# A fused attention and mixture-of-experts kernel: the first unit's second layer by parts, and the second mixture ahead of its loop

## The chip, the cores and the metric

The kernel runs on one core of a Trainium2 chip. The metric is device time in microseconds (us) of one execution. The time before is the median of three runs. Engines are named as in the profile: PE is TensorE (matmuls) and PEld its weight loads, DVE is VectorE, ACT is ScalarE, POOL is GpSimd, SP is SyncE, whose queue issues the DMAs; a name with a q behind it (SPq, PEldq) is the engine's sequencer.

## What is computed

Three stages follow each other: Nystrom attention, a gated layer, and a mixture of experts with a skip.

```python
def _attn_ref(q, k, v):                     # 4 x 8 heads, 576 tokens, 64 wide
    q_lm, k_lm = means of 18 neighbours     # 32 landmarks
    A, Bm, C = sm(q, k_lm), sm(q_lm, k_lm), sm(q_lm, k)
    Z = ...                                 # six steps of an iterative inverse of Bm
    return A @ Z @ C @ v

def _moe_ref(x, w_gate, w_val, w_out, rms_g):
    xn = x / sqrt(mean(x * x) + 1e-6) * rms_g
    g = xn @ w_gate                         # 512 -> 1536
    return (g * sigmoid(g) * (xn @ w_val)) @ w_out

def _moe2_ref(x, w_skip, w_gate, w1, w2):   # 8 experts
    do_compute = x @ w_skip > 0             # the other tokens are passed through
    e = argmax(x @ w_gate); p = softmax(x @ w_gate)[e]
    return x + p * (relu(x @ w1[e]) @ w2[e])
```

The first is in outline; the routing picks one expert for each token that is computed. The gated layer's weights come as 64-bit floats and are converted on the chip.

## The kernel before

The 2304 tokens are four batches of 576, and each batch is two **units** of 288 tokens. `run_unit(u)` (line 1179) does the gated layer of one unit: for each of twelve parts f of the hidden layer two groups of matmuls (`gemm`, into the PSUM tiles pg and pv) and their evictions, which leave a high and a low half in h_t; then the second layer. `project(c, ps, fs)` (line 875) adds parts fs of the hidden layer to output chunk c, one of four, in PSUM tile o, with three matmuls for each part (high by high, high by low, low by high). PSUM tiles pg, pv, o, ph and py share one pool of four banks (`accbank`).

The **second layer's weights** w_out are loaded and converted during unit 0, part by part (`convert_wout`, line 761: one load, operations on ScalarE and VectorE, then a high half from ScalarE and a low half from VectorE or GpSimd, alternately). In unit 0 all conversions left are named first (`drain(conv)`, line 1188), then the four chunks one after the other, each with all twelve parts, with a `slot()` after two parts.

`slot` (line 1161) lets side work (the conversions, the next batch's attention and weight products, the last unit's finish) be named between the matmuls. `Paced` adds up an estimate of each engine's busy time, and a slot stops as soon as an engine is more than SLACK = 700 ahead of TensorE. The order in which an engine runs its instructions is then laid down at compile time by a scheduler that goes by the order of naming and by when inputs are ready; each engine runs its own list in order.

The **mixture of experts** goes by pairs of an expert and a batch. `list_pairs` (line 968) makes a list of those that have tokens, with their number at its end (index 2 LP). `early` does this during unit 7, for the first three batches, so that one pair is known; `list_pairs("rest", ...)` lists the others when unit 7 is finished. `pair_at` loads an entry into registers of SyncE. `mixture(e, b, nxt, ahead)` (line 1084) does one pair with all 576 tokens of the batch: eight parts of a hidden layer (w2 of the pair split into halves, 24 matmuls into ph for each half of the tokens, then Relu on ScalarE and the low half on VectorE), the loads of the pair's routing weights mc and of the rows of the output (`load_rows`, line 1054), the loads and splits of the next pair's x and w1 and the loads of its w2, then the output matmuls (py), which VectorE scales by mc and adds to the rows, and the stores. mc is 0 for tokens that the pair doesn't serve.

The first pair runs as straight-line code; a loop over the others follows (`tc.For_i`, line 1337), whose count each engine loads into a register (`number`, line 1005). Between two passes of the loop stands a back edge, at which the engines wait for each other. Nearly all instructions carry line 58, that of a helper; loads and loop instructions have their own lines.

Of the kernel before, what the change touches and what calls it, by code (L numbers as in the profile page):

```python
# [62 lines left out]
def attention_moe_kernel(  # L63
# [75 lines left out]
    def accbank(name):  # L139
        return acc.tile([128, 512], F32, name=name, tag="acc")  # L140

    def bank(name):
        return pb.tile([128, 512], F32, name=name, tag="b")
# [824 lines left out]
    def list_pairs(name, but=None):  # L968

        pq = bank("pq")  # L970
        PE.matmul(
            pq[0:32, 0:1], Ms.rearrange("p b e -> p (b e)"), ones[:, 0:1],
            start=True, stop=True,
        )
        fl = rt.tile([32, 1], F32, name="fl")
        if but is None:
            V.tensor_scalar(fl, pq[0:32, 0:1], 0.0, None, ALU.is_gt)
        else:
            V.scalar_tensor_tensor(
                fl, pq[0:32, 0:1], 0.0, but, ALU.is_gt, ALU.subtract  # L980
            )
        pq = bank("pq")
        PE.matmul(pq[0:32, 0:1], tri, fl, start=True, stop=True)
        ps = rt.tile([32, 1], F32, name="slot")
        V.tensor_copy(ps, pq[0:32, 0:1])
        oh = const.tile([32, LP], F32, name=f"oh{name}")
        V.tensor_scalar(oh, pos, ps, fl, ALU.is_equal, ALU.mult)
        pl = bank("pl")
        PE.matmul(pl[0:1, 0:LP], pair[:, 1:2], oh, start=True, stop=True)
        PE.matmul(pl[0:1, LP : 2 * LP], pair[:, 2:3], oh, start=True, stop=True)  # L990
        PE.matmul(
            pl[0:1, 2 * LP : 2 * LP + 1], fl, ones[0:32, 0:1], start=True, stop=True
        )
        lst = const.tile([1, 2 * LP + 1], I32, name=name)
        V.tensor_copy(lst, pl[0:1, 0 : 2 * LP + 1])
        return lst, oh[:, 0:1]

    SPE = mybir.EngineType.SP

# [5 lines left out]
    def number(lst):  # L1005
        return nc.values_load(lst[0:1, 2 * LP : 2 * LP + 1], min_val=0, max_val=B * E)

    def pair_at(lst, i):
        return ld(lst, i, E - 1), ld(lst, i + LP, B - 1)
# [44 lines left out]
    def load_rows(e, b):  # L1054

        mc = late.tile([128, 5], F32, name="mc")
        mrow = m_d[bass.ds(b * S, S), bass.ds(e, 1)]
        with nc.allow_non_contiguous_dma(reason="one column"):
            SP.dma_start(
                mc[:, 0:4], mrow[0:512].rearrange("(t p) o -> p (t o)", p=128)  # L1060
            )
            SP.dma_start(mc[0:64, 4:5], mrow[512:576])
        orow = out[bass.ds(b * S, S), :]
        olds = []
        for t in range(5):
            m = 128 if t < 4 else 64
            old = late.tile([128, DM], F32, name=f"old{t}")
            SP.dma_start(old[0:m], orow[128 * t : 128 * t + m, :])
            olds.append(old)
        return mc, orow, olds  # L1070

    def early(res):

        lst, res["mark"] = list_pairs("lst")
        e, b = res["pair"] = pair_at(lst, 0)
        for c in range(KC):
            load_x(b, c, V if c % 2 else G)
        yield
        for i in range(2):
            for f in range(4 * i, 4 * i + 4):  # L1080
                load_w1(e, f, V if f % 2 else G)
            yield

    def mixture(e, b, nxt, ahead):

        hs = []
        for f in range(FC2):
            if ahead:
                r = w2raw(f)
            else:  # L1090
                r = late.tile([128, S], F32, name="w2r", tag="ld", bufs=4)[:, 0:DM]
                load_w2(e, f, r)
            rsplit(V if f % 2 else G, *w2s(f), r)
            wh, wl = (t.rearrange("p (c f) -> p c f", c=KC) for t in w1s(f))

            hh, hx, hl = (
                hroom[f][:, s] for s in (slice(0, S), slice(512, 640), slice(640, None))
            )
            for t in range(2):
                ts = slice(NH * t, NH * t + NH)  # L1100
                ps = accbank("ph")[:, 0:NH]
                for c in range(KC):
                    xh, xl = xs[0][:, c, ts], xs[1][:, c, ts]
                    PE.matmul(ps, wh[:, c], xh, start=(c == 0), stop=False)
                    PE.matmul(ps, wh[:, c], xl, start=False, stop=False)
                    PE.matmul(ps, wl[:, c], xh, start=False, stop=(c == KC - 1))
                A.activation(hh[:, ts], ps, AF.Relu)
                n = (NH, 512 - NH)[t]
                V.scalar_tensor_tensor(
                    hl[:, NH * t : NH * t + n], ps[:, 0:n], 0.0,  # L1110
                    hh[:, NH * t : NH * t + n].bitcast(F32), ALU.max, ALU.subtract,
                )
            V.scalar_tensor_tensor(
                hx[:, 64:128], ps[:, n:NH], 0.0, hx[:, 0:64].bitcast(F32),
                ALU.max, ALU.subtract,
            )
            hs.append((hh, hx, hl))
            if f == FC2 - 3:
                mc, orow, olds = load_rows(e, b)
            yield  # L1120
        en, bn = nxt()
        if not w2r_t:
            w2r_t.extend(wo_tile(F32) for _ in range(FC2 // 2))
        for c in range(KC):
            load_x(bn, c, V)
        for f in range(FC2):
            load_w1(en, f, V if f % 2 else G)
        for f in range(FC2):
            load_w2(en, f, w2raw(f))

        ps = accbank("py")
        for f in range(FC2):
            for i, w in enumerate(w2s(f)):
                PE.matmul(
                    ps, hs[f][1], w,
                    start=(f + i == 0), stop=(f + i == FC2),
                )
        old = olds[4][0:64]
        for p in (ps[0:64], ps[64:128]):
            V.scalar_tensor_tensor(old, p, mc[0:64, 4:5], old, ALU.mult, ALU.add)  # L1140
        SP.dma_start(orow[512:S, :], old)
        yield
        for t in range(4):
            ts = slice(128 * t, 128 * t + 128)
            old = olds[t]
            ps = accbank("py")
            for f in range(FC2):
                (hh, _, hl), (wh, wl) = hs[f], w2s(f)
                PE.matmul(ps, hh[:, ts], wh, start=(f == 0), stop=False)
                PE.matmul(ps, hh[:, ts], wl, start=False, stop=False)  # L1150
                PE.matmul(ps, hl[:, ts], wh, start=False, stop=(f == FC2 - 1))
            V.scalar_tensor_tensor(
                old, ps, mc[:, t : t + 1], old, ALU.mult, ALU.add
            )
            SP.dma_start(orow[ts, :], old)
            yield
# [4 lines left out]
    def slot():  # L1161

        for n in "VAG":
            busy[n] = max(busy[n], busy["P"])
        for g in side[:]:
            if max(busy[n] for n in "VAG") > busy["P"] + SLACK:
                break
            if next(g, "end") == "end":
                side.remove(g)

    def drain(g):
        for _ in g:
            pass
        if g in side:
            side.remove(g)
# [3 lines left out]
    def run_unit(u, before):  # L1179

        for f in range(FC):
            before(f)
            h = hidden_g(gemm(u % 2, f, "g"))
            slot()
            hidden_v(f, h, gemm(u % 2, f, "v"))
            slot()
        if u == 0:
            drain(conv)
        elif fin:
            drain(fin.pop())  # L1190
        x2T = x2T_tile(F32)
        for c in range(KC):
            ps = accbank("o")[:, 0:NH]
            for f in range(0, FC, 2):
                project(c, ps, (f, f + 1))
                slot()
            evacuate(x2T, c, ps)
        fin.append(finish(u, x2T))
        side.insert(0, fin[0])
# [117 lines left out]

    def others():
        yield from fin[0]
        rest.append(list_pairs("rest", first["mark"])[0])  # L1320
        yield

    oth = others()
# [2 lines left out]
    for g in side[:]:  # L1326
        drain(g)

    def after_first():
        drain(oth)  # L1330
        return pair_at(rest[0], 0)

    for _ in mixture(*first["pair"], after_first, False):
        next(oth, None)
        next(oth, None)
    npairs = number(rest[0])
    with tc.For_i(0, npairs) as i:  # L1337
        e, b = pair_at(rest[0], i)
        drain(mixture(e, b, lambda: pair_at(rest[0], i + 1), True))
    ph1.close()  # L1340
    ctx.close()

# [32 lines left out]
```

## Time and profile before

| | |
|---|---|
| median of 3 runs | 715.3 us (713.17 to 715.6) |
| the profiled execution | 715.35 us |
| its span in the trace | 713.6 us |
| mean granted clock of TensorE | 0.958 |
| TensorE busy | 651.2 us (91%) |
| VectorE busy | 471.5 us (66%) |
| ScalarE busy | 294.9 us (41%) |
| GpSimd busy | 145.6 us (20%) |

The profiled execution is longer than its span by 1.75 us, which lie around it. Times in the trace count from the start of the span. The granted clock is a share of full speed, 2.4 GHz; the other level is 1.2 GHz. The chain of waits follows what ended last back to what released it; a timeline merges neighbouring instructions of a kind and gives in brackets how long the engine was idle before them and what ended that.

### The profile page before, as it was taken

What the parts mean: (1) busy time and instruction counts of PE and PEld (TensorE: products, weight loads), DVE (VectorE), ACT (ScalarE), POOL (GpSimd) and SP (SyncE); (2) the same over time, 40 slices, a digit from 0 to 9 for tenths busy, and PEclk for the clock granted to TensorE, in tenths of its full rate; (3) what the DMA queues carried; (4) which work ended last, traced back from release to release, by engine and by line L of the source; (5) the groups of instructions that cost most, each with busy time, mean ns of one, the idle gap of its engine ahead of it and who ended that gap; (6) DMA issues with size and microseconds to landing.
All of it is one profiled execution on the core that took longest, in us unless ns stands there. A gap on an engine that the chain in (4) does not pass through costs nothing. (4 is left out here: it accounts for less than half of the span.)

```text
span 713.6 us, 13229 instructions
## 1 busy us (share of the span) xinstructions
PE 651.2 (91%) x4891; PEld 562.2 (79%) x4891; DVE 471.5 (66%) x1012; ACT 294.9 (41%) x637; POOL 145.6 (20%) x162
## 2 busy tenths in 40 slices
PE   5388599798999799999999999999999999997997
PEld 4366267687977598978898888999899988986985
DVE  6985999988987775888458968360634464352451
ACT  1864888834224421442441434340533253332240
POOL 4000035304200140320130230040542033022120
PEclk9766799999999999999999999999999999998999
DMA  9775644671246651229612208310641474372344
GB/s 310 244 238 204 222 180 153 196 186 51 88 99 134 187 133 51 84 75 206 159 36 67 80 6 178 93 37 1 184 127 63 147 234 148 106 235 81 119 143 160
DMA packets 79434, 97.10 MB, mean 136 GB/s; under 512 B 16016, under 2 KB 58000, under 8 KB 79376
## 3 DMA queue, kind: packets, MB, share of 16 engines
q1 hardware_dynamic: 79376, 96.33, 45.8%
q8 instruction: 36, 0.59, 0.3%
q14 instruction: 22, 0.18, 0.1%
HBM read 76.97 MB, written 19.34 MB: 135 GB/s over the span
## 5 line engine op out<-in xcount | busy, mean ns | idle before, releaser
L58 PE MATMUL o<-h_t,wo 128*128 128x288 f32 x1152 | 167.3, 301 | 6.7 <-ACT wo L58 3.1
L58 PEld LDWEIGHTS o<-h_t,wo 128*128 128x128 f32 x1152 | 156.7, 190 | 15.9 <-issue 6.3
L58 POOL TENSOR_TENSOR h_t<-h,h_t 128x288 fp32r<-128x288 f32 x96 | 82.4, 861 | 388.5 <-ACT h_t L58 364.1
L58 PE MATMUL pg<-ap_t,P 128*128 128x288 f32 x576 | 104.1, 307 | 11.2 <-ACT P L58 7.9
L58 PEld LDWEIGHTS pg<-ap_t,P 128*128 128x128 f32 x576 | 83.6, 191 | 24.4 <-issue 14.9
L58 PE MATMUL pv<-ap_t,P 128*128 128x288 f32 x576 | 99.1, 302 | 1.8 <-DVE h L58 0.8
L58 PEld LDWEIGHTS pv<-ap_t,P 128*128 128x128 f32 x576 | 83.2, 190 | 6.5 <-issue 2.2
L58 PE MATMUL ph<-xsh,P 128*128 128x288 f32 x384 | 80.2, 302 | 4.5 <-PEq L1337 4.5
L58 PEld LDWEIGHTS ph<-xsh,P 128*128 128x128 f32 x384 | 63.8, 194 | 5.4 <-issue 5.4
L58 DVE SCALAR_TENSOR_TENSOR h<-h,pg 128x288 f32<-128x288 f32 x96 | 42.7, 448 | 33.1 <-ACT h L58 32.3
L58 ACT ACTIVATE h<-pg 128x288 f32<-128x288 f32 x96 | 39.2, 411 | 49.3 <-PE pg L58 46.6
L58 PE MATMUL ph<-xsl,P 128*128 128x288 f32 x192 | 57.8, 301 | 0.0
L58 ACT CAST h_t<-h 128x288 fp32r<-128x288 f32 x96 | 41.0, 430 | 29.6 <-DVE h L58 28.8
L58 PE MATMUL py<-wo,h_t 128*128 128x512 f32 x210 | 51.4, 395 | 0.0
L58 PEld LDWEIGHTS py<-wo,h_t 128*128 128x128 f32 x210 | 39.5, 188 | 9.5
L58 DVE TENSOR_TENSOR h<-h,pv 128x288 f32<-128x288 f32 x96 | 42.7, 448 | 4.7 <-PE pv L58 1.3
L58 DVE STREAM_TRANSPOSE T<-kq 64x576 f32<-64x576 f32 (+1 forms) x40 | 35.5, 887 | 5.6 <-DMA kq<-in_k_dram 3.8
L58 ACT CAST P<-P 128x512 fp32r<-128x512 f32 x48 | 26.4, 585 | 27.2 <-PE P L58 26.5
L58 PEld LDWEIGHTS ph<-xsl,P 128*128 128x128 f32 x192 | 37.2, 194 | 0.1
L58 DVE TENSOR_TENSOR P<-P,P 128x512 fp32r<-128x512 f32 x48 | 31.9, 688 | 5.7 <-ACT P L58 5.4
L58 POOL TENSOR_TENSOR P<-w1r,P 128x512 fp32r<-128x512 f32 x16 | 21.1, 1318 | 66.6 <-ACT P L58 66.6
L58 DVE SCALAR_TENSOR_TENSOR old<-py,mc,old 128x512 f32<-128x512 f32 (+1 forms) x18 | 13.5, 749 | 31.3 <-PE py L58 31.0
(226 smaller groups left out, 957.1 us busy)
## 6 DMA issues: line engine op xcount, KB each, us to landing
wl<-wg_d SPq DMA_DIRECT2D x36, 256.0 KB, 4.5
wr<-wv_d SPq DMA_DIRECT2D x32, 256.0 KB, 4.7
w1r<-in_moe_w_dram SPq DMA_DIRECT2D x32, 256.0 KB, 3.5
wr<-in_moe_w_gate_dram SPq DMA_DIRECT2D x6, 1024.0 KB, 6.3
wr<-in_moe_w_val_dram SPq DMA_DIRECT2D x6, 1024.0 KB, 5.9
wo<-in_moe_w_dram SPq DMA_DIRECT2D x24, 256.0 KB, 5.3
kq<-in_k_dram SPq DMA_DIRECT2D x8, 576.0 KB, 4.0
kq<-in_q_dram SPq DMA_DIRECT2D x8, 576.0 KB, 3.8
```

The source lines that it names most:

```text
L58: return f(*args, **kw)
```

## The change

In unit 0 the second layer takes four PSUM tiles at once, and goes part by part: when part f of w_out has been converted, its three matmuls are named for each of the four chunks. The slots lie between them, two for each part. For the other units the order stays.

The second mixture is taken out of the loop and stands as straight-line code between the first mixture and the loop. The loop's count, at the end of the list, becomes one less (at least 0), and its entries are read one further on. As there may be only one pair in all, `list_pairs` makes a factor that is 1 if the list has an entry and 0 if not, on all 128 partitions, and the second mixture multiplies its mc by it.

```diff
         lst = const.tile([1, 2 * LP + 1], I32, name=name)
-        V.tensor_copy(lst, pl[0:1, 0 : 2 * LP + 1])
-        return lst, oh[:, 0:1]
+        V.tensor_copy(lst[:, 0 : 2 * LP], pl[0:1, 0 : 2 * LP])
+
+        V.tensor_scalar(
+            lst[:, 2 * LP :], pl[0:1, 2 * LP : 2 * LP + 1], 1.0, 1.0,
+            ALU.max, ALU.subtract,
+        )
+        pn = bank("pn")
+        PE.matmul(
+            pn[:, 0:1], fl.to_broadcast([32, 128]), ones[0:32, 0:1],
+            start=True, stop=True,
+        )
+        any_ = rt.tile([128, 1], F32, name="any")
+        V.tensor_scalar(any_, pn[:, 0:1], 1.0, None, ALU.min)
+        return lst, oh[:, 0:1], any_
...
-    def mixture(e, b, nxt, ahead):
+    def mixture(e, b, nxt, ahead, any_=None):
...
                 mc, orow, olds = load_rows(e, b)
+                if any_ is not None:
+                    V.tensor_scalar(mc[:, 0:4], mc[:, 0:4], any_, None, ALU.mult)
+                    V.tensor_scalar(
+                        mc[0:64, 4:5], mc[0:64, 4:5], any_[0:64], None, ALU.mult
+                    )
...
+        if fin:
+            drain(fin.pop())
         if u == 0:
+
+            pss = [accbank("o")[:, 0:NH] for c in range(KC)]
+            for f in range(FC):
+                while len(wo_t) <= f:
+                    next(conv)
+                for c, ps in enumerate(pss):
+                    project(c, ps, (f,))
+                    if c % 2:
+                        slot()
             drain(conv)
-        elif fin:
-            drain(fin.pop())
         x2T = x2T_tile(F32)
         for c in range(KC):
-            ps = accbank("o")[:, 0:NH]
-            for f in range(0, FC, 2):
-                project(c, ps, (f, f + 1))
-                slot()
+            if u == 0:
+                ps = pss[c]
+            else:
+                ps = accbank("o")[:, 0:NH]
+                for f in range(0, FC, 2):
+                    project(c, ps, (f, f + 1))
+                    slot()
             evacuate(x2T, c, ps)
...
-        rest.append(list_pairs("rest", first["mark"])[0])
+        rest.extend(list_pairs("rest", first["mark"])[0::2])
...
+    second = []
+
     def after_first():
         drain(oth)
-        return pair_at(rest[0], 0)
+        second.append(pair_at(rest[0], 0))
+        return second[0]
...
+    drain(mixture(*second[0], lambda: pair_at(rest[0], 1), True, rest[1]))
     npairs = number(rest[0])
     with tc.For_i(0, npairs) as i:
-        e, b = pair_at(rest[0], i)
-        drain(mixture(e, b, lambda: pair_at(rest[0], i + 1), True))
+        e, b = pair_at(rest[0], i + 1)
+        drain(mixture(e, b, lambda: pair_at(rest[0], i + 2), True))
```

## Rows read from the trace of the kernel before

**Rows 1.** The page: span; busy time and share of engines; one costly group.

```profile
span 713.6 us, 13229 instructions
PE 651.2 (91%) x4891; PEld 562.2 (79%) x4891; DVE 471.5 (66%) x1012; ACT 294.9 (41%) x637; POOL 145.6 (20%) x162
...
L58 PE MATMUL ph<-xsh,P 128*128 128x288 f32 x384 | 80.2, 302 | 4.5 <-PEq L1337 4.5
```

**Rows 2.** The chain of waits, where it begins: start us, us, what.

```profile
654.69 0.28 issue
654.97 27.93 PE ph L58 x192
```

**Rows 3.** PE's timeline around the back edge: start us, us, group, count, idle before.

```profile
646.83 3.66 PE L58 MATMUL py<-wo,h_t 128*128 128x512 f32 x15
654.97 0.58 PE L58 MATMUL ph<-xsh,P 128*128 128x288 f32 x1 [4.49 <-PEq L1337]
...
659.19 0.68 PE L58 MATMUL ph<-xsh,P 128*128 128x288 f32 x2
659.91 0.43 PE L58 MATMUL ph<-xsh,P 128*128 128x288 f32 x2
660.32 0.43 PE L58 MATMUL ph<-xsh,P 128*128 128x288 f32 x2
```

**Rows 4.** PE's timeline: loop entry, and the last output matmuls of the third mixture.

```profile
595.21 3.66 PE L58 MATMUL py<-wo,h_t 128*128 128x512 f32 x15
598.71 0.30 PE L58 MATMUL ph<-xsh,P 128*128 128x288 f32 x1
...
705.38 3.66 PE L58 MATMUL py<-wo,h_t 128*128 128x512 f32 x15
```

**Rows 5.** Windows: length, busy us (count) of engines, PEclk, DMA share, GB/s.

```profile
655.00:660.00 5.00, 5.00 (x21) 5.00 (x22) 3.65 (x4) 3.80 (x8) 3.67 (x3) 0.51 0.23 43
...
709.05:713.60 4.55, 0.00 (x0) 0.00 (x0) 0.75 (x1) 0.00 (x0) 0.00 (x0) 0.73 0.17 61
```

**Rows 6.** Lines 1006 and 1337 (ns min/median/max, first and last start), and stores: KB, landing.

```profile
L1006 PEldq TENSOR_LOAD <-rest x1: 753/753/753, 594.5 to 594.5; - x1
...
L1337 SPq EVENT_SEMAPHORE  x19: 17/17/28, 652.1 to 654.6; - x19
...
out_dram<-old SPq DMA_DIRECT2D x7, 256.0 KB, 2.0
```

**Rows 7.** Small operations by tile: duration ns min/median/max, first and last start.

```profile
L58 PE MATMUL pq<-ones,Ms x4: 167/170/191, 500.0 to 558.9; 128*32 128x1 f32 x4
...
L58 DVE TENSOR_SCALAR nmx<-mx x8: 174/210/214, 17.0 to 393.4; 128x1 f32<-128x1 f32 x8
```

**Rows 8.** Second mixture: SP's timeline, landing of mc, and an eviction on ACT's timeline.

```profile
603.03 0.55 SPq L1062 DMA_DIRECT2D mc<-m_d  x1
...
608.20 2.08 SPq L1051 DMA_DIRECT2D x2r<-xT_d  x4
...
mc<-m_d SPq DMA_DIRECT2D x1, 0.2 KB, 1.9
...
605.28 0.41 ACT L58 ACTIVATE P<-ph 128x288 fp32r<-128x288 f32 x1 [1.19 <-PE ph L58]
```

**Rows 9.** Unit 0's second layer: timelines of PE and DVE, windows as in rows 5.

```profile
116.68 1.48 PE L58 MATMUL o<-h_t,wo 128*128 128x288 f32 x10
118.75 3.72 PE L58 MATMUL o<-h_t,wo 128*128 128x288 f32 x26 [0.59 <-POOL wo L58]
...
145.99 0.79 PE L58 MATMUL o<-h_t,wo 128*128 128x288 f32 x4 [0.68 <-DVE wo L58]
...
145.26 0.67 DVE L58 TENSOR_TENSOR wo<-x,wo 128x512 fp32r<-128x512 f32 x1
...
132.00:138.40 6.40, 5.77 (x28) 5.30 (x28) 5.93 (x11) 5.54 (x10) 3.17 (x2) 0.73 0.57 194
...
116.60:146.80 30.20, 23.54 (x148) 21.15 (x147) 28.99 (x44) 22.40 (x38) 10.97 (x8) 0.94 0.61 184
```

More of the change, by code (lines that the diff above doesn't have):

```diff
@@ L1072, in early @@
     def early(res):
-        lst, res["mark"] = list_pairs("lst")
+        lst, res["mark"], _ = list_pairs("lst")
         e, b = res["pair"] = pair_at(lst, 0)
```

## Prediction

> **What bounds the kernel now.** I read the page first: TensorE is busy 91% of a span of 713.6 us, so a change pays where it closes a hole in TensorE's stream, and elsewhere mostly not [rows 1]. Then the chain of waits: it runs back over the last mixture alone, from its output matmuls (py) to its hidden matmuls (ph, 27.93 us), and stops at 654.69, just after an idle stretch [rows 2]. The table of groups says how often a mixture ran: one has 8 x 2 x 4 x 2 = 128 products with xsh, 384 are counted, so three pairs have tokens [rows 1]. The first is the straight-line one; the loop ran twice.
>
> TensorE's own timeline then shows the two borders between the three mixtures, and they differ. From the first to the second (entry into the loop) there is none: the last output matmuls begin at 595.21 and end at 598.87, and the second mixture's first starts at 598.71 [rows 4]. From the second to the third (the loop's back edge) they end at 650.49, and the next starts at 654.97, after 4.49 us put down to the sequencer at L1337 [rows 3]. SyncE's events of that line run from 652.1 to 654.6, behind the last store (2.0 us from issue to landing); at the entry TensorE's queue read the loop count at 594.5, under matmuls that were still running [rows 6]. After the hole matmuls run at half pace: groups of three lie 0.72 us apart until 659.91 and 0.41 us from then on, and the granted clock of 655 to 660 is 0.51: that is the lower level, 1.2 GHz, until the pace of the upper one, 2.4 GHz, sets in [rows 3, 5].
>
> For the other part I read TensorE's timeline of unit 0's second layer, 116.68 to 146.78 us, and a window over it [rows 9].
>
> **The change part by part.** *The second mixture ahead of the loop.* The loop is now entered before the third mixture and its count is 2 - 1 = 1, so the back edge is not taken. What goes: the third mixture would start where an entry lets it, 0.16 us before the end of the last output matmul as in [rows 4], at 650.33 instead of 654.97, so 4.64 us. It also starts on an engine that has not stood still. The second mixture takes from 598.71 to 650.49, 51.78 us; the third takes from 654.97 to 709.04, 54.07 us [rows 3, 4]. The difference, 2.29 us, is the slow start. Together 6.93 us. What stays: the loop's exit, 4.55 us from the last matmul to the end of the span with the last eviction and store in it, happens once before and once after [rows 5].
>
> The moved mixture issues the same matmuls, evictions and DMAs as a pass of the loop: loads of the third pair's x, w1 and w2 and of its own rows. On SyncE they stand behind the first mixture's stores, as they do now, since the loop's first pass is queued behind those too. Its w2 splits now already begin before TensorE leaves the first mixture, so a common block has no hole to fill there: value 0, bounds from no gain to 0.16 us of lost overlap.
>
> *The lists.* Both lists get one matmul (fl broadcast over 128 columns) and two small VectorE operations: the count, split from the copy, and the minimum. The nearest matmul row is pq at 0.17 us, two passes for one matmul; I take 0.25 us per list of TensorE's time between its neighbours (between 0.17 and twice that), so 0.5 us for both lists, because TensorE is the bound around them [rows 7]. The VectorE operations cost about 0.21 us each by the nearest one-column operation [rows 7]. VectorE is not the bound at either place. SyncE's register loads wait for the list, and the loads of x behind them come up to 0.5 us later, tens of us before the mixture that reads them. Value 0, at worst those 0.5 us.
>
> *The guard.* Two VectorE operations multiply mc in the second mixture, about 0.21 us each [rows 7]. This is an added wait: VectorE is held until mc has landed, and queued behind it are the hidden splits, which release the PSUM banks that TensorE's next hidden matmuls need. In the loop's first pass the second mc load was issued at 603.03 and took 1.9 us, so mc is there at 604.9 [rows 8]. TensorE fills one bank each 1.60 us, the distance of ScalarE's evictions (0.41 us and 1.19 us of idle), and has four: starting at 598.71 it runs dry at 605.1 at the earliest, if VectorE did nothing at all from then [rows 4, 8]. So value 0; the bound above, with VectorE held from the first mixture's last eviction to 604.9 and one split of half a us after it, is 0.5 us.
>
> *Unit 0's second layer.* The code goes from chunk by chunk (all twelve parts of one output chunk) to part by part through four accumulators. But TensorE's stream is already by parts: 10 and 26 matmuls, 36 = 3 parts x 4 chunks x 3, stand before the wait for the fourth part, and after the last wait, for VectorE's split of the last part (145.26 + 0.67), only 4 are left [rows 9]. That is one per chunk, the least that can be left. The matmuls are placed as their inputs come, whatever order the code names them in. What sets the end is the conversion of w_out, and there VectorE is busy 28.99 of 30.20 us [rows 9]. The change takes no operation from VectorE or ScalarE there, and the pacing in `slot` hardly brings attention forward between the parts: by the constants of Paced a part charges VectorE with at least 3 x (60 + 1.05 x 512) = 1793 and its 12 matmuls charge TensorE with 12 x (10 + 0.47 x 288) = 1744, so VectorE's account, once further ahead than SLACK, stays there. Value 0. Bounds: a gain of 1.2 us if VectorE's idle time went, or of up to 5 us if attention's transposes and sums were put behind the conversion (ScalarE has 22.40 of 30.20 us there, and a part of its idle is the tail behind the last cast); a loss of 8 x 0.14 = 1.1 us if all twelve matmuls of the last part stood behind its split [rows 9].
>
> Sum, against the profiled execution (713.6 us of span and 1.75 us around it, 715.35 us, which is the median of 715.3 to a hair): 715.35 - 4.64 - 2.29 + 0.5 = 708.9 us.
>
> **The rivals.** *The entry is not free behind a straight-line second mixture*, and the hole only moves. For it: TensorE's queue read the count only some 4 us ahead of the end of the last matmul [rows 4, 6]. Against: the same entry, behind the same sort of mixture, is measured without a hole. It would give back both terms: 715.35 + 0.5 = 715.9 us.
>
> *TensorE slows down in unit 0's second layer.* Going round four banks with short idles between the groups, it would run at the lower level. Groups of three at 0.72 us make 144 matmuls last 34.6 us where they take 30.1 now: 4.5 us more, 713.4 us [rows 3, 9]. The Trainium skill speaks for this rival: "TensorE: Matmul & The Clock Gate", section "A second HAM failure mode: psum-queue depth-cycling", tells of a kernel that cycled through banks, idled briefly between groups, and lost the full clock again and again. The trace does not bear that out: TensorE goes through four banks in this layer already, with short waits between the groups, and the granted clock of the whole layer is 0.94; it is low in one stretch alone (0.73, from 132), behind a wait of 2.52 us [rows 9].
>
> *The guard holds VectorE up*, the one that ends slower. If the straight-line schedule puts the two mc loads behind the four x loads on SyncE, which in the loop were issued until 610.3 [rows 8], they land at about 613.2. With the guard ahead of the splits, TensorE, dry at 605.1, goes on at about 613.7: 8.6 us of hole and 2.3 us of slow start, 719.8 us. It decides against the kernel as soon as mc lands later than about 608.8, since the hole then eats the 6.4 us gained. Against it: the loads of the rows are named ahead of those of the next x, and the traced pass issues them so, 5 us ahead [rows 8].
>
> *Unit 0's layer gains after all*, 2 to 5 us of the bound above, and keeps it: about 705.5 us. Against: VectorE has to do attention's work in any case, and is nearly full behind the layer too.
>
> **How the numbers follow.** Forecast 0.82 (708.9 us), hole moved 0.06, slow clock 0.03, guard 0.03, gain in unit 0 0.06. The forecast's own range takes in 1.1 us from the order in unit 0, 0.5 us from the guard, 0.2 us from the lists and some 0.8 us of scatter above, and 1.2 us from unit 0 with 1.2 us of half the scatter of the three runs (713.17 to 715.6) below: 706.5 to 711.5. Down to 705.5 it takes in the gain in unit 0, and leaves out some 0.15. A measurement can tell about 0.5%, 3.6 us, from no change. Faster by more, under 711.7 us: the forecast and the gain, 0.88. Within: hole moved and slow clock, 0.09. Slower: the guard, 0.03.
>
> **What would show it.** In the changed kernel's trace the wait of TensorE for its sequencer at the loop's line is gone, the hidden matmuls behind the second mixture start with the last output matmuls of it, at 2.4 GHz, and the three mixtures lie without a hole. Unit 0's layer still ends about 30 us after its start, with VectorE's last split just before the last few matmuls. It is wrong if a hole or a slow start of some us stands ahead of the second or third mixture, if VectorE is idle behind mc's DMA while TensorE waits for a split, or if unit 0's layer is shorter or longer than now by more than 2 us.

## The result, and the profile after

| | before | changed |
|---|---|---|
| median, side by side | 715.3 us (713.17 to 719.54) | 710.7 us (709.24 to 713.02) |
| the profiled execution | 715.35 us | 709.24 us |
| its span | 713.6 us | 707.5 us |
| from the first ph to the last py (three mixtures) | 165.43 us | 159.10 us |
| from there to the end of the span | 4.56 us | 5.13 us |
| mean granted clock | 0.958 | 0.962 |

The ratio of the times is 0.9915 (95% interval 0.9892 to 0.9938): faster by 0.6 to 1.1%. The forecast was 708.9 us, in a range of 705.5 to 711.5. Between the medians lie 4.6 us and between the two profiled executions 6.1, where the sum had 6.43.

First the page of the changed kernel, which answers to [rows 1]: its span and engines, and the group of the hidden matmuls, with its mean in ns and the idle time ahead of it in the last column.

```profile
span 707.5 us, 13185 instructions
PE 648.8 (92%) x4895; PEld 559.5 (79%) x4895; DVE 471.1 (67%) x1018; ACT 296.5 (42%) x637; POOL 146.1 (21%) x162
...
L58 PE MATMUL ph<-xsh,P 128*128 128x288 f32 x384 | 78.1, 296 | 0.0
```

There are still 384 of these matmuls, so three pairs ran. The 4.5 us of idle time put down to PE's sequencer are gone, and the mean fell from 302 to 296 ns. Next the timeline of PE at both borders and at the end (start us, us, group, count, idle before in brackets), which answers to [rows 3, 4].

```profile
595.28 3.68 PE L58 MATMUL py<-wo,h_t 128*128 128x512 f32 x15
598.79 0.29 PE L58 MATMUL ph<-xsh,P 128*128 128x288 f32 x1
...
646.98 3.68 PE L58 MATMUL py<-wo,h_t 128*128 128x512 f32 x15
650.50 0.29 PE L58 MATMUL ph<-xsh,P 128*128 128x288 f32 x1
650.63 0.29 PE L58 MATMUL ph<-xsl,P 128*128 128x288 f32 x1
650.76 0.43 PE L58 MATMUL ph<-xsh,P 128*128 128x288 f32 x2
...
698.69 3.68 PE L58 MATMUL py<-wo,h_t 128*128 128x512 f32 x15
```

At 650.50 the third mixture begins 0.16 us before the end of the second one's last output matmul (646.98 + 3.68 = 650.66). No row there has a bracket, and the matmuls keep the quick pace from the first one on. The windows say the same of the clock: the second mixture, a stretch just behind the border, and the exit. The columns are those of [rows 5].

```profile
598.95:650.66 51.71, 51.71 (x307) 46.57 (x306) 20.95 (x42) 16.92 (x34) 10.08 (x8) 1.00 0.46 150
655.00:660.00 5.00, 5.00 (x40) 5.00 (x39) 3.22 (x8) 1.34 (x4) 1.33 (x1) 1.00 0.40 106
...
702.40:707.50 5.10, 0.00 (x0) 0.00 (x0) 0.75 (x1) 0.00 (x0) 0.00 (x0) 0.76 0.15 56
```

The granted clock of 655 to 660 is 1.00, where it was 0.51 [rows 5]. The chain of waits (start us, us, what) no longer stops at the last border:

```profile
572.72 26.23 PE py L58 x112
598.95 25.47 PE ph L58 x192
624.42 26.23 PE py L58 x112
650.66 25.47 PE ph L58 x192
676.13 26.25 PE py L58 x112
```

It runs over TensorE alone through all three mixtures: the last ph stretch is 25.47 us, where it was 27.93 [rows 2]. In parts: the first mixture, from its start to that of the second, went from 55.10 to 55.52 us (+0.42). The second, from its first hidden matmul to the end of its last output matmul, went from 51.78 to 51.87 (+0.09), and the third, counted in the same way, from 54.07 to 51.87 (-2.20). The border between these two, from the end of one to the start of the other, went from 4.48 to -0.16 (-4.64). That makes -6.33. The exit took 0.57 more, and the part ahead of the mixtures 0.34 less (543.61 to 543.27): -6.1 us, the difference of the spans.

The new operations of the lists and of the guard, by PE's and VectorE's timelines, answer to [rows 7, 8].

```profile
560.61 0.19 PE L58 MATMUL pl<-ones,fl 32*1 32x1 f32 x2
560.73 0.38 PE L58 MATMUL pn<-ones,fl 32*128 32x1 f32 x2
561.04 0.40 PE L58 MATMUL ph<-xsl,P 128*128 128x288 f32 x1
...
603.58 0.23 DVE L58 TENSOR_SCALAR mc<-mc,any 128x4 f32<-128x4 f32 x1 [0.45 <-DMA mc<-m_d]
604.04 0.21 DVE L58 TENSOR_SCALAR mc<-mc,any 64x1 f32<-64x1 f32 x1 [0.23 <-DMA mc<-m_d]
```

The list's matmul is two passes and takes 0.31 us from its start to that of the next hidden matmul. VectorE did wait for mc at the guard, 0.45 and 0.23 us, and PE had no wait at that time.

Last, unit 0's second layer: PE's timeline, VectorE's last split and the windows, which answer to [rows 9].

```profile
116.79 4.93 PE L58 MATMUL o<-h_t,wo 128*128 128x288 f32 x36
123.19 2.21 PE L58 MATMUL o<-h_t,wo 128*128 128x288 f32 x14 [1.47 <-ACT wo L58]
...
132.12 10.34 PE L58 MATMUL o<-h_t,wo 128*128 128x288 f32 x50 [2.53 <-ACT wo L58]
142.68 2.70 PE L58 MATMUL o<-h_t,wo 128*128 128x288 f32 x18 [0.22 <-POOL wo L58]
146.13 0.80 PE L58 MATMUL o<-h_t,wo 128*128 128x288 f32 x4 [0.75 <-DVE wo L58]
...
145.39 0.68 DVE L58 TENSOR_TENSOR wo<-x,wo 128x512 fp32r<-128x512 f32 x1
...
116.60:146.80 30.20, 24.54 (x148) 22.29 (x146) 28.98 (x44) 22.37 (x39) 11.12 (x8) 0.89 0.62 185
132.00:138.40 6.40, 6.19 (x24) 5.84 (x25) 6.06 (x12) 5.55 (x11) 3.06 (x2) 0.50 0.58 195
```

It lasts from 116.79 to 146.93, 30.1 us as before. Again 36 matmuls stand in front of the first longer wait and 4 behind the last, and VectorE and ScalarE are as busy as they were (28.98 and 22.37 us). The small wait of 0.59 us inside the first 36 is gone, and behind the wait of 2.53 us the clock is 0.50 where it was 0.73. Neither moves the end: the last four matmuls wait for VectorE's last split (145.39 + 0.68).

### The profile page after: what moved, and what is told of

It is laid out like the page before. It is cut to its first block, busy times and chain, and to the rows that moved or that the text cites. A ratio compares the mean times of both kernels' runs of the same rounds, so it can differ in the third digit from the quotient of the medians.

```text
span 707.5 us, 13185 instructions
## 1 busy us (share of the span) xinstructions
PE 648.8 (92%) x4895; PEld 559.5 (79%) x4895; DVE 471.1 (67%) x1018; ACT 296.5 (42%) x637; POOL 146.1 (21%) x162
## 4 chain that ended last, share of the span: by engine, by line
PE 71%; DVE 13%; DMA 6%; issue 4%; ACT 3%; POOL 2%; SPq 1%; POOLq 0%; ACTq 0%; DVEq 0%
PE o L58 16%; PE py L58 11%; PE ph L58 11%; PE pv L58 9%; PE pg L58 9%; PE P L58 3%; DVE wo L58 2%; PE sq L58 2%; PE nr L58 2%; DVE rbs L58 2%; DMA wr<-wv_d 2%; PE sk L58 2%; DVE ln L58 1%; DMA kq<-in_q_dram 1%; DMA wl<-wg_d 1%
## 5 line engine op out<-in xcount | busy, mean ns | idle before, releaser
L58 PE MATMUL ph<-xsh,P 128*128 128x288 f32 x384 | 78.1, 296 | 0.0
L58 PEld LDWEIGHTS ph<-xsh,P 128*128 128x128 f32 x384 | 62.0, 188 | 0.6 <-issue 0.5
L58 DVE SCALAR_TENSOR_TENSOR h_t<-ph,h_t 128x288 fp32r<-128x288 f32 (+2 forms) x45 | 14.7, 353 | 27.8 <-ACT h_t L58 27.8
```

The source lines that it names most:

```text
L58: return f(*args, **kw)
```

## The experiments

All times below are medians beside runs of the kernel before on the same chip, whose medians were 716.2 us for the changed kernel again, for each half alone and for the third mixture, 715.8 for the two repeated ones, and 716.6 for the other four.

### The changed kernel again

The profiled execution of the changed kernel was 1.4 us below its median, so the kernel was run once more as it is.

> The changed kernel once more, on the chip of the next three, so that they can be set beside it. Both theories: 709 to 713 us, with a ratio to the kernel before of 0.989 to 0.994. The profile tells whether the 1.4 us between the first profiled execution (709.24 us) and the median of its seven runs (710.68 us) lies at one place: theory A, ahead of the mixtures (unit 0 or the start), so that the three mixtures take 51.7 us each again; theory B, at the loop's exit, which took 5.1 us from the last matmul where 4.6 were seen before.

Measured: 710.5 us, ratio 0.9912 (0.9886 to 0.9938). Its profiled execution has a span of 709.8 us, 2.3 more than the first, and the mixtures take 159.11 us (545.52 to 704.63), as in the first. Unit 0's first gated matmul starts at 85.2 us instead of 82.85. The exit takes 5.2 us, as long as in the first, so it is not what separates them: that lies ahead of the first gated matmul, and not in the changed stages.

### The second mixture alone ahead of the loop

Unit 0's second layer goes back to the order of the kernel before.

```diff
...
-            pss = [accbank("o")[:, 0:NH] for c in range(KC)]
-            for f in range(FC):
...
+            ps = accbank("o")[:, 0:NH]
+            for f in range(0, FC, 2):
+                project(c, ps, (f, f + 1))
+                slot()
```

> The second mixture ahead of the loop, unit 0's second layer as before. Theory: the whole gain is here, so the time is that of the changed kernel within 0.7 us (709 to 711.5 us), with no hole ahead of the third mixture. Rival: the order by parts adds a gain or a loss of its own, and this kernel stands at least 1.2 us from the changed one.

Measured: 712.8 us, ratio 0.9939 (0.9917 to 0.9961). Mixtures 159.11 us, unit 0's layer 30.1 us, as in the changed kernel. The median is 2.2 us above that of the changed kernel beside it. Taken by itself this is the rival's result (at least 1.2 us apart), but the trace had no place for it but the start (first gated matmul at 87.17 us). So the two were run again, side by side:

> The second mixture alone ahead of the loop, as in the run e1 (unit 0 as in the kernel before), to see whether its median, 2.2 us above that of the changed kernel in the first comparison, is its own. Theory A (unit 0's part is worth nothing): the median lies within 0.7 us of the changed kernel's that runs beside it, and the mixtures take 159.1 us in both. Theory B (unit 0's part is worth some 2 us in a way that the one profiled execution did not show): it lies 1.5 to 3 us above again.

> The changed kernel as it is, beside the run with the second mixture alone, for their comparison on one chip. Theory A: both medians within 0.7 us, the ratio to the kernel before 0.991 to 0.993 for both. Theory B: this one 1.5 to 3 us below the other.

Measured: 712.5 us (709.4 to 716.12), ratio 0.9932 (0.9907 to 0.9957), for the second mixture alone, and 713.0 us (711.34 to 713.38), ratio 0.9943 (0.9922 to 0.9963), for the changed kernel. They are 0.5 us apart, in the other direction this time, and the mixtures take 159.10 and 159.30 us. Both ratios came out above what was expected (0.991 to 0.993). The 2.2 us of the first comparison did not come back, so they are taken as scatter, and the mixture alone carries the gain, as far as comparisons with a scatter of some 2 us can tell. In the trace these two start late as well: the first gated matmul at 87.75 and 87.22 us. Not all scatter lies ahead of that point, though: the mixtures of the first begin at 550.04 us and those of the second at 547.02.

### Unit 0's part alone

The kernel before, with the new order of unit 0's second layer, and the loop as it was.

> Unit 0's second layer by parts, the loop as before. Theory: no change, 715.3 us within 0.7, the layer from 116.7 to 146.9 us, its last four matmuls behind VectorE's last split, and the hole of 4.5 us with 2.3 us of slow start behind the second mixture. Rival: the new order costs something, since the granted clock of the layer fell from 0.94 to 0.89 with it: 716.5 us or more. Another rival: it gains 1.2 us or more.

Measured: 716.95 us, ratio 1.0014 (0.9993 to 1.0035): no change, that is, between 0.5 us faster and 2.5 us slower. The number by itself lies outside the 0.7 us of the theory and meets the first rival (716.5 us or more), but the kernel before was at 716.2 beside it. PE's timeline at the back edge is that of the kernel before:

```profile
647.04 3.66 PE L58 MATMUL py<-wo,h_t 128*128 128x512 f32 x15
655.20 0.58 PE L58 MATMUL ph<-xsh,P 128*128 128x288 f32 x1 [4.50 <-PEq L1349]
```

The layer takes 30.1 us (117.2 to 147.3). So this half of the change is worth nothing that can be seen, from both sides: with it removed the layer takes the same 30.1 us and the time moved by +2.2 and -0.5 us in two comparisons; put alone into the kernel before it gains nothing.

### Unit 0's layer held to its named order

Why is it worth nothing? The prediction said that the scheduler had put these matmuls in order by parts before. Here the kernel before keeps TensorE to the order of naming, chunk by chunk. The edit also leaves out the slots between these matmuls in unit 0, so the side work that they let in is named elsewhere; what that alone does isn't separated.

```diff
+        if u == 0:
+            pss = [accbank("o")[:, 0:NH] for c in range(KC)]
+            with tc.manual_schedule(engines={nc.tensor.engine}):
+                for c in range(KC):
+                    project(c, pss[c], range(FC))
...
```

> The kernel before with unit 0's second layer held to the order in which its code names it: all twelve parts of one output chunk, then the next. Theory: the layer by parts in the kernel before was the scheduler's doing; held to the named order TensorE stands through the conversions with one chunk, and the other three chunks, 108 matmuls of 0.133 us, come behind the last split: 14 us later than now, 729 us, more if the clock falls. Rival: the order doesn't matter, since the conversions leave TensorE enough time: 715 us.

Measured: 734.4 us, ratio 1.0265 (1.0201 to 1.0329), 17.8 us more than before. PE's timeline, its end:

```profile
143.64 0.85 PE L58 MATMUL o<-h_t,wo 128*128 128x288 f32 x2 [0.77 <-ACT wo L58]
145.61 17.55 PE L58 MATMUL o<-h_t,wo 128*128 128x288 f32 x109 [1.12 <-DVE wo L58]
163.00 0.53 PE L58 MATMUL pb<-lmk,bdq 128*128 128x32 f32 x4
```

The first chunk creeps along with the conversion until 145.61, and then 109 matmuls are left, 108 of them the other three chunks. They take 17.55 us, 0.161 each. That is the layer which the source of the kernel before describes, and which its trace didn't have: the scheduler had already done by itself what the change writes out. The layer's end came 16.4 us later than before (163.16 instead of 146.78), where 14 were expected, since these matmuls took 0.161 us each, at a granted clock of 0.82, and not the 0.133 of the expectation. The spans of the two profiled executions lie 18.1 us apart (731.7 and 713.6); the rest of that was not followed up.

### What the layer waits for

In the changed kernel the conversion of w_out leaves out the sign, two operations on ScalarE and one on VectorE for each part; the values of w_out are then wrong, and the rest is as it was.

> The changed kernel with the sign left out of the conversion of w_out (two ScalarE operations and one VectorE operation less for each of the twelve parts; the values of w_out are then not the reference's). Theory: the end of unit 0's second layer is set by the conversion, which loses 12 x (0.75 + 0.72) = 18 us of ScalarE and 12 x 0.6 = 7 us of VectorE: the layer's end comes 5 to 12 us earlier from the kernel's start, and the whole kernel gains most of it. Rival: TensorE's order or its clock sets the end, and it moves by less than 2 us.

Measured: 710.4 us, ratio 0.9916 (0.9889 to 0.9943): as the changed kernel. The layer shrank from 30.1 to 27.1 us (118.9 to 146.0). But the expectation was about its end, and that came only 0.9 us earlier than in the changed kernel (146.93), or 1.9 us counted from unit 0's first gated matmul (83.77 and 82.85). This is the rival's number, less than 2 us, though not for the rival's reason: the granted clock of the layer is 1.00, and the last matmuls wait for VectorE's last split again (timelines of VectorE and PE):

```profile
141.93 2.19 DVE L58 TENSOR_REDUCE ln<-kq 128x64 f32<-128x1152 f32 x1 [1.76 <-DMA kq<-in_k_dram]
144.04 0.68 DVE L58 TENSOR_TENSOR wo<-x,wo 128x512 fp32r<-128x512 f32 x1
...
144.78 1.20 PE L58 MATMUL o<-h_t,wo 128*128 128x288 f32 x7 [0.58 <-DVE wo L58]
```

That split stands behind a sum of the next batch's attention, which waited 1.76 us for its load of k. In the same window as above, 30.20 us long, VectorE is busy for 27.41 us instead of 28.98 and ScalarE for 13.56 instead of 22.37. Unit 1's layer ends 4.3 us earlier (215.4 instead of 219.7). But unit 2's layer starts at 258.1 us, and at 258.2 in the changed kernel. The chain of the changed kernel in between shows loads of weights for the next batch:

```profile
225.97 6.58 DMA wr<-wv_d
...
235.34 5.20 DMA wr<-wv_d
```

In the lighter kernel PE waits there for operations of VectorE on P (2.25 and 2.42 us):

```profile
234.61 1.69 PE L58 MATMUL P<-wl,WT 64*32 64x256 f32 x32 [2.25 <-DVE P L58]
238.72 1.19 PE L58 MATMUL lp<-x2T,wcat 128*32 128x288 f32 x8 [2.42 <-DVE P L58]
```

The lighter conversion shortened the layer by 3 us, but moved its end by less than 2 of the 5 to 12 us expected, and what was gained by the end of unit 1's layer is gone before unit 2's. The statement that most of the gain would be kept fell. The prediction's bound of 5 us for a gain in unit 0 was therefore too wide: what VectorE and ScalarE saved there did not reach the kernel's end. Which wait takes it back was read from the two traces and not tested.

### One more back edge

In the changed kernel the count of the loop is raised by one, so that a pass for an empty entry of the list follows the third mixture.

```diff
-            lst[:, 2 * LP :], pl[0:1, 2 * LP : 2 * LP + 1], 1.0, 1.0,
+            lst[:, 2 * LP :], pl[0:1, 2 * LP : 2 * LP + 1], 1.0, 0.0,
```

> The changed kernel with the loop's count one higher: a pass more, over a list entry behind the end, so that its additions to the output are not the reference's. It brings the back edge back between two passes and nothing else. Theory: the pass itself takes 51.7 us as the three others, and the back edge adds its hole of 4.6 us and its slow start of 2.3 us: 58.6 us above the changed kernel, about 768 to 771 us, with the hole ahead of the fourth pass alone. Rival: what was saved was not the back edge, and the added pass costs 52 us, without a hole.

Measured: 771.7 us, the median of two executions (769.53 and 773.85), 0.7 us above the range expected. The mixtures take 218.25 us, 59.15 more than in the changed kernel. PE's timeline at the back edge:

```profile
699.84 3.68 PE L58 MATMUL py<-wo,h_t 128*128 128x512 f32 x15
708.00 0.58 PE L58 MATMUL ph<-xsh,P 128*128 128x288 f32 x1 [4.48 <-PEq L1370]
...
713.66 0.57 PE L58 MATMUL ph<-xsh,P 128*128 128x288 f32 x2
...
714.20 0.42 PE L58 MATMUL ph<-xsh,P 128*128 128x288 f32 x2
```

A mixture without a border behind it takes 51.72 us, so the back edge costs 59.15 - 51.72 = 7.43 us here. At the border 4.64 us are lost, the 4.48 of the hole and the overlap of 0.16; and the fourth mixture takes 54.63 us (708.00 to 762.63), 2.76 more than the third of the changed kernel, for its slow matmuls last until 713.66 this time. Put back in, the back edge costs about what was gained by taking it out (4.64 and 2.20 us), and the hole has the same length with other passes around it.

### Is it the idle time or the branch that slows the third mixture?

The kernel before gets 12 matmuls more at the end of each pass of the loop; they read tiles that are there anyway, and nobody reads their result.

```diff
+        if ahead:
+            for k in range(2):
+                ps = accbank("fill")
+                for f in range(6):
+                    (hh, _, hl), (wh, wl) = hs[f], w2s(f)
+                    PE.matmul(ps, hh[:, 384:512], wh, start=(f == 0), stop=(f == 5))
```

> The kernel before with twelve matmuls more at the end of each pass of the loop, into a bank that nobody reads, 12 x 0.233 = 2.8 us: they keep TensorE going while the last eviction and store run, and end before the store has landed. Theory: the back edge takes the same time, so the third mixture starts where it did (some 656 us at the same start), but after an idle stretch of some 1.7 us instead of 4.5; if the slow start comes from the idle stretch, part or all of it goes and the third mixture takes nearer to 51.8 than 54.1 us: 0 to 2.3 us gained. Rival: the slow start belongs to the branch, and the third mixture takes 54.1 us as before. Against both: the exit's or the back edge's barrier waits for the added matmuls, and the time rises by up to 2.8 us.

Measured: 714.2 us, ratio 0.997 (0.9941 to 1.0). The interval reaches up to no change, so the trace has to tell. PE's timeline:

```profile
647.30 3.66 PE L58 MATMUL py<-wo,h_t 128*128 128x512 f32 x15
...
652.90 0.86 PE L58 MATMUL fill<-wo,h_t 128*128 128x512 f32 x3
655.45 0.37 PE L58 MATMUL ph<-xsh,P 128*128 128x288 f32 x1 [1.70 <-PEq L1345]
...
655.80 0.42 PE L58 MATMUL ph<-xsh,P 128*128 128x288 f32 x2
656.06 0.29 PE L58 MATMUL ph<-xsl,P 128*128 128x288 f32 x1
656.19 0.43 PE L58 MATMUL ph<-xsh,P 128*128 128x288 f32 x2
```

The border is as long as it was: from the end of the last output matmul (647.30 + 3.66 = 650.96) to the next hidden one it is 4.49 us. But PE has been idle for 1.70 us only, and the groups of three lie 0.40 us apart at once, at a granted clock of 1.00 up to 660. The third mixture takes 51.86 us instead of 54.07, and the three together 163.26 us, 2.17 less than before. The two terms of the sum are two different things: the wait at the border, which the fill leaves as it is, and the lower clock behind a long idle stretch, which work without a use removes.

### The third mixture ahead of the loop too

The same step once more, so that the loop makes no pass with this input. The count in the list becomes two less, and `list_pairs` makes a second factor for the third mixture.

```diff
...
+    drain(mixture(*second[0], after_second, True, rest[1]))
+    drain(mixture(*third[0], lambda: pair_at(rest[0], 2), True, rest[2]))
```

> The third mixture ahead of the loop too, whose count is then 0. Theory: in the changed kernel the border ahead of the third mixture has no hole left, and the loop's exit ends with the landing of the last store, so only what comes behind that landing can be gained: 0 to 1 us against the changed kernel. Rival: the exit's barrier itself costs about what the back edge cost, and this kernel gains 2 us or more. Rival on the other side: skipping the loop's body means a jump over its code, and costs 1 us or more.

Measured: 711.15 us, ratio 0.9938 (0.9916 to 0.996), no better than the changed kernel (710.5 us beside it). The mixtures take 159.14 us (542.05 to 701.19), but from there to the end of the span it takes 8.1 us, 3.0 more than in the changed kernel. The events at the loop's line (ns min/median/max, first and last start):

```profile
L1380 SPq EVENT_SEMAPHORE  x17: 17/17/28, 702.6 to 708.2; - x17
...
L1380 PEldq COMPARE_BRANCH  x3: 101/193/3428, 697.5 to 705.7; - x3
```

One branch of PE's queue, the jump over the loop, started at 701.4 and took 3.43 us; the other engines' last events at this line come at 705 or later, behind it. That is not all of the 3.0 us: SyncE's queue has a branch at 705.2, no further event until 707.8, and its last event at 708.2, when PE's last branch (705.7) is long past. What SyncE waits for there was not tested. The second rival, a jump that costs 1 us or more, is borne out by this trace; the medians, 0.6 us apart, can't tell it from scatter. The entry that was free was free in the runs in which the loop is entered, and a border moved past the last mixture was not had for nothing.

## Why the prediction was right

**The hole** (forecast -4.64): -4.64, from the end of one mixture to the start of the next. The entry into the loop behind a straight-line second mixture costs what it did behind the first, nothing [rows 4]; the rival in which the hole only moves is out. The extra pass shows the other side: with a back edge the same kernel has 4.48 us of hole again.

**The slow start** (forecast -2.29): -2.20 in the changed kernel, and -2.17 from the first to the last matmul of the three mixtures where the fill alone removed it. That it comes from standing still was argued from [rows 3, 5], and the fill shows it.

**The lists** (forecast +0.25 each): mis-sized, a little. The first mixture, in which one of them is made, got 0.42 us longer, of which 0.31 is seen at the new matmul. The length by itself proves little: in unit 0's part alone, without the new matmul, the first mixture takes 55.54 us too, there with a wait of 0.21 us for VectorE. The other list lies in unit 7, where the executions differ by more than that; its cost can't be told.

**The guard** (forecast 0, bound 0.5): VectorE waited 0.7 us for mc and TensorE not at all. The loads of mc went out ahead of the next pair's x, at 601.4 and 602.1, 1 us earlier than before. The slower rival, in which they come late, did not happen.

**Unit 0's second layer** (forecast 0, bounds from -5 to +1.1): 0, by three runs. The reading of 36 and 4 matmuls in [rows 9] as an order by parts was right; held to the order of the source, the kernel loses 17.8 us. The rival with a slow clock did not come: the layer did not get longer. The granted clock of the layer fell from 0.94 to 0.89, and to 0.50 in the stretch behind the wait of 2.53 us. But the same stretch of other kernels, in windows of 7.5 us, shows that this doesn't go with the order. First the second mixture alone, which has the old order, then unit 0's part alone, which has the new one:

```profile
136.00:143.50 7.50, 7.00 (x28) 6.45 (x28) 6.35 (x12) 6.24 (x11) 3.85 (x2) 0.54 0.64 200
```

```profile
132.00:139.50 7.50, 5.77 (x28) 5.30 (x28) 6.49 (x12) 6.38 (x11) 3.71 (x2) 0.77 0.61 196
```

The clock (the third number from the end) is 0.54 with the old order and 0.77 with the new one, and the layer takes 30.1 us in both: TensorE has time there until VectorE's last split. It doesn't go with the code of this layer either: the kernel with the fill has that of the kernel before, and shows 0.50 in the 6.40 us behind its wait of 2.52 us, where the kernel before shows 0.73. What sets the clock apart is open. The Trainium skill, "TensorE: Matmul & The Clock Gate", section "A second HAM failure mode: psum-queue depth-cycling", ties a loss of throughput to cycling through banks with short idles between the groups. Here the clock does fall in such a stretch, behind a wait of 2.5 us, but with both orders, and no time is lost by it.

**The exit** was taken as unchanged, and that is the one term that failed, by 0.57 us: 4.56 us before and 5.13 after. All profiled executions with the second mixture ahead and a loop that is entered have 5.0 to 5.2 us; unit 0's part alone and the fill, with the loop as it was, have 4.57 and 4.59. The extra pass has 5.2 too, so the number of passes isn't the cause. VectorE's last event at the loop's line comes at 706.0 us, half a us behind that of SyncE and ScalarE (705.5); in the kernel before they came within 0.2 us, at 712.1 to 712.3. In the changed kernel:

```profile
L1370 DVEq EVENT_SEMAPHORE  x8: 50/50/50, 702.6 to 706.0; - x8
L1370 SPq EVENT_SEMAPHORE  x8: 28/28/28, 703.8 to 705.5; - x8
L1370 ACTq EVENT_SEMAPHORE  x6: 38/38/38, 700.0 to 705.5; - x6
```

What holds VectorE's queue there isn't settled; no run separates it.

**The sum**: -4.64 - 2.20 + 0.09 + 0.42 + 0.57 - 0.34 = -6.1, against -6.43. The medians moved by 4.6 us, 5.7 and 2.7 us in the three comparisons of this kernel. One source of that is seen in the profiled executions of all these kernels: unit 0's first gated matmul starts up to 5 us apart (82.61 to 87.75 us). The -0.34 for the part ahead of the mixtures is within that scatter too, and not an effect of the change. The range gave the scatter 0.8 us above the forecast, and that was too little: the first two medians lie 1.6 to 1.8 us above 708.9, the third 4.1 us and outside the range. The first stayed inside with the help of the 1.1 us that stood there for the order in unit 0, which cost nothing; that much was luck.

## What to carry to other kernels

Look at every border between passes of a loop on the timeline of the bounding engine, and price a back edge by two rows: the idle time that the sequencer ends, and the slow stretch behind it, which was gone here after 1.70 us of idle time instead of 4.49. A pass taken out of the loop in front paid as long as the loop was still entered. With an input of only two pairs the changed kernel's loop would have the count 0 as well, and no back edge to save; going by the run with the third mixture it would then lose some us, but no run had such an input. And before an order is written out by hand, read from the trace the order that the engine really runs: here it was already the better one, and only holding the scheduler to the source made the difference visible.

## What the chip showed besides

- Jumping over a loop whose count is 0 took a branch of 3.43 us on PE's queue, while entering it cost PE nothing (the next matmul starts 0.16 us before the last one ends), and leaving it after a pass took a branch of 0.32 us on the same queue. The Trainium skill, "Runtime: NRT & Kernel Launch", section "Instruction fetch mechanics", says that a taken branch to code outside the fetched window waits for its fetch. The 3.43 us fit that; that they are a fetch was not shown.
- PE kept 2.4 GHz over an idle stretch of 1.70 us at the back edge, and came out of 4.48 to 4.50 us at 1.2 GHz every time (the kernel before, unit 0's part alone, the extra pass), for 4.9 to 5.7 us of matmuls.
- With less work for VectorE and ScalarE in unit 0, unit 1's second layer ended 4.3 us earlier (215.4 instead of 219.7 us), and unit 2's still began at the same time (258.1 and 258.2).
